# Attention products in float32 instead of high and low parts, two heads side by side in the array

## The chip, the cores and the metric

The kernel runs on one core of one Trainium2 chip. A core has TensorE (matrix products, results in PSUM), VectorE, ScalarE and GpSimd for element-wise work, and SyncE (SP), whose queue issues the DMAs. Time is device microseconds from start to end of one execution. Before the change it is 2203.7 us, the median of three runs (2202.99 to 2203.8).

## The reference

An attention layer with a compressed memory, then a mixture of eight experts and a plain two-layer network. Cut to what matters here:

```python
B, H, S, D = (4, 8, 576, 64)
scores = scale * np.matmul(q, k.transpose(0, 1, 3, 2))
scores = np.where(causal, -1000000000.0, scores)
scores = scores - scores.max(-1, keepdims=True)
a = np.exp(scores)
a /= a.sum(-1, keepdims=True) + 1e-09
local = np.matmul(a, v)
q_p = phi(q)                                  # elu + 1
mem_ret = np.einsum('bhsd,bhde->bhse', q_p, M_prev)
mem_norm = np.einsum('bhsd,bhd->bhs', q_p, z_prev)[..., None] + 1e-06
g = 1.0 / (1.0 + np.exp(-beta))[None, :, None, None]
x = g * (mem_ret / mem_norm) + (1 - g) * local
# then: gate of x with 8 rounds of row and column normalization,
# 8 experts of 512 -> 1024 -> 512 on all 2304 tokens, and 512 -> 2048 -> 512
```

All arrays are float32.

## The kernel before

Heads go in pairs: 4 batches of 4 pairs are 16 pairs, the two heads of a pair on partitions 0 to 63 and 64 to 127. `Attention.run` is a generator that records the work of one pair after the other; `yield` hands back control, so that the caller can put other work in between.

**Precision.** The products are made of operands in float32r, a float32 of fewer bits. Each operand `x` is cut into a high part (`hi`, a copy into a float32r tile, mostly on ScalarE) and a low part (`lo = x - hi`, on GpSimd or VectorE), and a product of two operands is the sum of high by high, high by low and low by high. `split` does it for q and k (lines 131 to 141), `values` for v and the memory matrix (175 to 185), `turned` for the features, `turn` for the probabilities.

**One pair** runs through four stages of query rows: blocks 0 and 1 of 128 rows, block 2, block 3, and the last 64 rows of both heads (`STAGES`). In a stage, `turn` transposes the probabilities of the pair before (TensorE into `atps`), with the high part taken out by ScalarE (`ath`) and the low part by VectorE (`atl`); `scores` makes the products of this pair into `sps`; `softmax` adds the mask and finds the row minimum on VectorE (line 214) and takes exponentials with row sums on ScalarE (line 216). The scores of heads 0 and 1 use 64 rows of the array each:

```python
for i, (x, y) in enumerate(((qh, kh), (qh, kl), (ql, kh))):
    for j in range(2):
        s, o = slice(j * D, (j + 1) * D), 512 * j + 256 * n
```

For the last stage both heads' 64 queries stand as a block-diagonal matrix `bd`, on all 128 rows. After the stages `normalize` divides by the row sums (lines 220 to 227; its first instruction writes `sm`, once a pair). `outputs` multiplies for the pair before, one head at a time: the stationary operand is 128 columns wide, 64 of v's high part and 64 of its low part, so the high parts' sum comes out on one half of the partitions and the low parts' on the other, and `collect` adds the halves into `x` (lines 279 and 285). `turned` transposes the features `nq` into `tps` (line 170).

**What sets the order.** The engines take their instructions in the order of a scheduler that runs over the recorded program. Pairs 0 to 3 run with nothing but the weight conversion of the first expert beside them (`W`, lines 465 and 466). From then on each `yield` of the attention lets `fill` put in up to two units of the first expert's work (`First.run`: `ph`, line 499, and `po`, line 507; four units are a step on 256 tokens), as the table says:

```python
FILL = {1: 1, 2: 2, 4: 2, 5: 2, 7: 2}
```

A pair of heads so takes 16 units, 4 steps. Of First's 72 steps 48 stand beside the attention; the others stand in the gate and the normalization after it. Then come the other experts (`rest`, lines 812 to 881), which take most of the time and are not touched.

Of the kernel before, what the change touches and what calls it, by code (L numbers as in the profile page):

```python
# [60 lines left out]
class Attention:  # L61
# [6 lines left out]
    def __init__(self, tc, ctx, xh, xl, xd, qt, kt, qn, vn, M_prev, z_prev, ident, g_bc, iomg_bc):  # L68
# [25 lines left out]
        self.at = [self.sb.tile([P, 2, self.WIDE], F32R, name=f"at{part}") for part in "hl"]  # L94
        self.qk = {n: [self.sb.tile([P, S], F32R, name=f"{n}{part}") for part in "hl"] for n in "qk"}
        self.bd = [self.sb.tile([P, P], F32R, name=f"bd{part}") for part in "hl"]
        self.ms = [self.sb.tile([P, P], F32R, name=f"ms{j}") for j in range(2)]
        for t in self.bd:
            nc.gpsimd.memset(f32(t), 0.0)
        for j, t in enumerate(self.ms):  # L100
            nc.gpsimd.memset(f32(t[D - j * D:P - j * D]), 0.0)
        for t in self.at:
            nc.vector.memset(f32(t[:, :, 1024:1152]), 0.0)
            nc.vector.memset(f32(t[:, :, 1344:1472]), 0.0)
# [7 lines left out]
    def load_qk(self, r):  # L112
        for nm, src in (("q", self.qt), ("k", self.kt)):
            r["raw" + nm] = self.sbt([P, S], "raw" + nm)
            self.nc.sync.dma_start(out=r["raw" + nm], in_=src[r["b"], r["hp"]])
# [8 lines left out]
    def load_v(self, r):  # L124
        b, hp = r["b"], r["hp"]
        r["v"] = self.sbt([P, 2, 5, D], "nv")
        self.nc.sync.dma_start(out=r["v"], in_=self.vn[b, hp])
        r["m"] = self.sbt([P, D], "nm")
        self.nc.sync.dma_start(out=r["m"], in_=self.M[b, 2 * hp:2 * hp + 2].rearrange("h p d -> (h p) d"))

    def split(self, r):

        nc = self.nc
        for n in "qk":
            (hi, lo), raw = self.qk[n], r["raw" + n]
            nc.scalar.activation(hi, raw, AF.Copy)
            nc.gpsimd.tensor_sub(lo, raw, f32(hi))
        for t, x in zip(self.bd, self.qk["q"]):
            for j in range(2):
                s = slice(j * D, (j + 1) * D)  # L140
                nc.gpsimd.tensor_copy(t[s, s], f32(x[s, 512:]))
# [33 lines left out]
    def values(self, r):  # L175

        nc = self.nc
        vs = r["vs"] = self.sbt([P, 10, P], "vs", F32R)
        v = r["v"].rearrange("p j c d -> p (j c) d")
        nc.vector.tensor_copy(vs[:, :, :D], v)  # L180
        nc.gpsimd.tensor_sub(vs[:, :, D:], v, f32(vs[:, :, :D]))
        for j, ms in enumerate(self.ms):
            s = slice(j * D, (j + 1) * D)
            nc.gpsimd.tensor_copy(ms[s, :D], r["m"][s])
            nc.gpsimd.tensor_sub(ms[s, D:], r["m"][s], f32(ms[s, :D]))

    def scores(self, r, ts):
# [3 lines left out]
        (qh, ql), (kh, kl) = self.qk["q"], self.qk["k"]  # L191
        if ts == (4,):
            qh, ql = self.bd
            for o, k0, kn in ((192, 0, 320), (512, 320, 256)):
                for i, (x, y) in enumerate(((qh, kh), (qh, kl), (ql, kh))):
                    nc.tensor.matmul(ps[:, o:o + kn], x, y[:, k0:k0 + kn], start=(i == 0), stop=(i == 2))
            return
        for n, t in enumerate(ts):
            w = max((t + 1) * P, 256)
            for i, (x, y) in enumerate(((qh, kh), (qh, kl), (ql, kh))):  # L200
                for j in range(2):
                    s, o = slice(j * D, (j + 1) * D), 512 * j + 256 * n
                    nc.tensor.matmul(ps[:, o:o + w], x[s, t * P:(t + 1) * P], y[s, :w], start=(i == 0), stop=(i == 2))
# [29 lines left out]
    def turn(self, r, ts):  # L233
# [26 lines left out]
    def outputs(self, r, j):  # L260
        nc = self.nc
        av = r["av"] = self.big("avps")
        rows = slice(j * D, (j + 1) * D)
        vs, ms, at = r["vs"], self.ms[j], self.at

        def group(o, q0, nq, parts):
            for i, p in enumerate(r["pT"]):
                nc.tensor.matmul(av[:, o:o + nq], ms, p[:, q0:q0 + nq], start=(i == 0), stop=False)
            for i, (c, s0, sn) in enumerate(parts):
                for k, t in enumerate(at):  # L270
                    nc.tensor.matmul(av[:, o + nq - sn:o + nq], vs[:, 5 * j + c, :], t[:, j, s0:s0 + sn], start=False,  # L271
                                     stop=(i == len(parts) - 1 and k == 1))

        group(256, 0, 256, ((0, 1600, 256), (1, 1344, 256)))
# [901 lines left out]
```

## Time and profile before

| | before |
|---|---|
| median of the runs | 2203.7 us |
| the profiled execution | 2206.66 us, span 2204.9 us |
| TensorE busy | 2131.9 us, 97% |
| VectorE busy | 1498.6 us, 68% |
| ScalarE busy | 821.8 us, 37% |
| GpSimd busy | 1183.0 us, 54% |
| mean granted TensorE clock | 0.987 |

PE is TensorE's products, PEld its weight loads, DVE VectorE, ACT ScalarE, POOL GpSimd. A row `avps<-ath,vs` names the tile that is written and those that are read. The shares over the whole span say little on the change, since the attention ends at 387 us; the stretches before that have to be read by themselves. An instruction's busy time holds its latency, and products overlap, so the distance between two starts is what a product costs. A true float32 product stands as two records in the trace.

### The profile page before, as it was taken

To read this page: it belongs to the slowest core of one execution; us is meant where nothing else is said; L and a number is where in the kernel's file an instruction comes from. 1 tells how busy PE (TensorE), PEld (TensorE's weight loads), DVE (VectorE), ACT (ScalarE), POOL (GpSimd) and SP (SyncE) were. 2 spreads that over 40 slices of the span, in tenths; PEclk is the share of its full clock that TensorE was granted. 3 is DMA by queue.
4 is the path that set the end of the run, shared out by engine and by line. 5 is a ranking of instruction groups with operands and counts; after the bars stand their busy time and mean duration, and the time that the engine had idled before them with its cause. 6 is when DMAs were issued, how large, how long until landed. Compare 5 with 4: busy or idle time off the path is not lost.

```text
span 2204.9 us, 35500 instructions
## 1 busy us (share of the span) xinstructions
PE 2131.9 (97%) x13781; PEld 1899.0 (86%) x13781; DVE 1498.6 (68%) x2666; ACT 821.8 (37%) x1645; POOL 1183.0 (54%) x1151
## 2 busy tenths in 40 slices
PE   5799999889999999999999999999999999999999
PEld 4688888789888899899889989889889898888998
DVE  7977776648776777777776898755555553566565
ACT  6777776233332222222222333333322333332421
POOL 7545443356774544444444678855554544564550
PEclk8899999999999999999999999999999999999999
DMA  4333331234532212212225444411111151326111
GB/s 148 99 100 104 106 107 54 82 107 153 154 119 67 67 58 72 88 58 67 68 68 205 159 136 125 131 58 58 39 58 58 39 221 58 114 89 237 57 58 39
DMA packets 161512, 214.17 MB, mean 97 GB/s; under 512 B 11072, under 2 KB 108352, under 8 KB 159808
## 3 DMA queue, kind: packets, MB, share of 16 engines
q1 hardware_dynamic: 161344, 211.90, 30.2%
q8 instruction: 109, 1.79, 0.3%
q14 instruction: 59, 0.48, 0.1%
HBM read 162.55 MB, written 49.28 MB: 96 GB/s over the span
## 4 chain that ended last, share of the span: by engine, by line
PE 74%; DVE 5%; issue 3%; POOL 3%; ACT 1%; DMA 1%; POOLq 0%; DVEq 0%; ACTq 0%
PE po L867 37%; PE pq L824 28%; PE pq L812 4%; PE po L507 1%; PE ph L499 1%; PE avps L271 1%; DVE hl L843 1%; POOL w0l L614 0%; DMA xa<-xd 0%; DVE acc L877 0%; DVE c L845 0%; PE atps L247 0%; DVE c L834 0%; POOL ql L614 0%; PE xt L929 0%
## 5 line engine op out<-in xcount | busy, mean ns | idle before, releaser
L867 PE MATMUL po<-w,hh 128*128 128x512 f32 x2592 | 810.6, 393 | 9.0 <-DVE acc L877 4.1
L867 PEld LDWEIGHTS po<-w,hh 128*128 128x128 f32 x2592 | 473.9, 188 | 107.3 <-DVE acc L877 3.4
L867 PE MATMUL po<-w,hl 128*128 128x512 f32 x1296 | 509.3, 393 | 0.0
L614 POOL TENSOR_TENSOR w0l<-raw,w0h 128x512 fp32r<-128x512 f32 x144 | 191.3, 1349 | 360.2 <-ACT w0h L613 359.7
L842 ACT ACTIVATE hh<-c 128x512 fp32r<-128x512 f32 x224 | 129.2, 624 | 477.5 <-DVE c L837 477.5
L867 PEld LDWEIGHTS po<-w,hl 128*128 128x128 f32 x1296 | 243.5, 188 | 56.1
L824 PE MATMUL pq<-Xh,w0h 128*128 128x256 f32 x960 | 266.2, 277 | 2.2 <-DVE uv L832 1.4
L824 PE MATMUL pq<-Xl,w0h 128*128 128x256 f32 x960 | 265.3, 276 | 0.0
L824 PE MATMUL pq<-Xh,w0l 128*128 128x256 f32 x960 | 265.1, 276 | 0.0
L843 DVE SCALAR_TENSOR_TENSOR hl<-c,hh 128x512 fp32r<-128x512 f32 x224 | 169.6, 798 | 79.2 <-ACT hh L842 79.2
L877 DVE SCALAR_TENSOR_TENSOR acc<-po,Pm,acc 128x512 f32<-128x512 f32 x252 | 178.4, 748 | 48.9 <-PE po L867 47.0
L614 POOL TENSOR_TENSOR w<-raw,w 128x512 fp32r<-128x512 f32 x144 | 199.8, 1405 | 3.3 <-ACT w L613 3.3
L832 DVE TENSOR_TENSOR uv<-pq,s 128x256 f32<-128x256 f32 x144 | 60.4, 420 | 193.8 <-ACT s L831 193.5
L824 PEld LDWEIGHTS pq<-Xh,w0h 128*128 128x128 f32 x960 | 180.1, 188 | 7.3 <-DVE uv L832 1.8
L824 PEld LDWEIGHTS pq<-Xl,w0h 128*128 128x128 f32 x960 | 180.2, 188 | 4.2
L824 PEld LDWEIGHTS pq<-Xh,w0l 128*128 128x128 f32 x960 | 180.2, 188 | 0.0
L831 ACT ACTIVATE s<-pq 128x256 f32<-128x256 f32 x144 | 54.8, 381 | 255.5 <-PE pq L824 255.4
L614 POOL TENSOR_TENSOR ql<-raw,qh 128x512 fp32r<-128x512 f32 x48 | 62.6, 1325 | 131.3 <-ACT qh L613 131.3
L846 ACT ACTIVATE hh<-c 128x512 fp32r<-128x512 f32 x64 | 40.5, 632 | 185.7 <-DVE c L845 185.7
L824 PE MATMUL pq<-Xh,w1h 128*128 128x256 f32 x384 | 106.1, 276 | 1.1 <-ACT xa L942 1.1
L824 PE MATMUL pq<-Xl,w1h 128*128 128x256 f32 x384 | 106.0, 276 | 0.0
L824 PE MATMUL pq<-Xh,w1l 128*128 128x256 f32 x384 | 106.0, 276 | 0.0
(274 smaller groups left out, 5395.8 us busy)
## 6 DMA issues: line engine op xcount, KB each, us to landing
raw<-in_moe_w_dram SPq DMA_DIRECT2D x136, 512.0 KB, 3.6
Xh<-kh SPq DMA_DIRECT2D x6, 1792.0 KB, 7.5
Xl<-kl SPq DMA_DIRECT2D x6, 1792.0 KB, 11.6
f<-in_moe_w_in_dram SPq DMA_DIRECT2D x16, 512.0 KB, 5.0
f<-in_moe_w_out_dram SPq DMA_DIRECT2D x16, 512.0 KB, 4.9
raw<-wide_in SPq DMA_DIRECT2D x16, 512.0 KB, 3.8
raw<-wide_out SPq DMA_DIRECT2D x16, 512.0 KB, 3.8
kh<-sth SPq DMA_DIRECT2D x12, 512.0 KB, 5.1
```

What stands on the lines that cost most here:

```text
L271: nc.tensor.matmul(av[:, o + nq - sn:o + nq], vs[:, 5 * j + c, :], t[:, j, s0:s0 + sn], start=False, stop=(i == len(parts) - 1 and k == 1))
L499: nc.tensor.matmul(ph[:, :T], wp[:, c, f0:f0 + P], x[:, c, t0:t0 + T], start=(n == 0), stop=(n == 11))
L614: self.nc.gpsimd.tensor_sub(lo, src, f32(hi))
L812: nc.tensor.matmul(ph[:, f * SB:(f + 1) * SB], wp(a, c % 2), xp[x][:, c], start=(n == 0), stop=(n == 11))
L824: nc.tensor.matmul(b[-1][:, o:o + SB], wp(a, c), X[s][part][:, x, c], start=(n == 0), stop=(n == 5))
L831: nc.scalar.activation(s1, b[0][:, lo], AF.Copy)
L832: v.tensor_add(uv[:, 0], b[0][:, up], s1)
L842: nc.scalar.activation(hh[:, f], c, AF.Relu)
L843: v.scalar_tensor_tensor(out=hl[:, f], in0=c, scalar=0.0, in1=f32(hh[:, f]), op0=ALU.max, op1=ALU.subtract)
L846: nc.scalar.activation(hh[:, f], c, AF.Copy)
L867: nc.tensor.matmul(po[j], a[:, f, r], w[1, part][:, f], start=(fp == 0 and f == 0 and n == 0), stop=(fp == 1 and f == 1 and n == 2))
L877: nc.vector.scalar_tensor_tensor(out=acc[t], in0=po[j], scalar=Pm[:, t0 + t, e:e + 1], in1=acc[t], op0=ALU.mult, op1=ALU.add)
```

## The change

All attention products are made with float32 operands, in one product where there were two or three. `split`, `values`, `collect` and the low parts are gone. q, k, v and the memory matrix are used as they are loaded, in two buffers each; `bd` is loaded from memory instead of copied. The scores keep the row halves, but with blocks cut to their own width (128 columns where 256 were taken). The outputs of both heads go into one `av` tile, head 0 in columns 0 to 63 of the array and head 1 in columns 64 to 127, each with its own moving operand; one copy by ScalarE takes both heads' `x`. Of the four evacuations of transposed probabilities VectorE makes two, ScalarE two.

```diff
-        self.at = [self.sb.tile([P, 2, self.WIDE], F32R, name=f"at{part}") for part in "hl"]
+        self.at = self.sb.tile([P, 2, self.WIDE], F32, name="at")
+        self.bd = [self.sb.tile([P, P], F32, name=f"bd{i}") for i in range(2)]
+        self.ms = [[self.sb.tile([P, D], F32, name=f"ms{j}{i}") for j in range(2)] for i in range(2)]
...
     def load_qk(self, r):
+            r[nm] = self.sbt([P, S], nm, bufs=2)
+            nc.sync.dma_start(out=r[nm], in_=src[b, hp])
+        r["bd"] = self.bd[hp % 2]
+        for j in range(2):
+            s = slice(j * D, (j + 1) * D)
+            nc.sync.dma_start(out=r["bd"][s, s], in_=self.qt[b, hp, s, 512:])
...
-        hi, lo = r["pT"] = [self.sbt([P, S], "pT" + part, F32R) for part in "hl"]
-        nc.scalar.activation(hi, ps[:, P:P + S], AF.Copy)
-        nc.vector.tensor_sub(lo, ps[:, P:P + S], f32(hi))
+        r["pT"] = self.sbt([P, S], "pT")
+        nc.scalar.activation(r["pT"], ps[:, P:P + S], AF.Copy)
...
     def scores(self, r, ts):
-            w = max((t + 1) * P, 256)
-            for i, (x, y) in enumerate(((qh, kh), (qh, kl), (ql, kh))):
-                for j in range(2):
-                    s, o = slice(j * D, (j + 1) * D), 512 * j + 256 * n
-                    nc.tensor.matmul(ps[:, o:o + w], x[s, t * P:(t + 1) * P], y[s, :w], start=(i == 0), stop=(i == 2))
+            w = (t + 1) * P
+            for j in range(2):
+                s, o = slice(j * D, (j + 1) * D), 512 * j + 256 * n
+                nc.tensor.matmul(ps[:, o:o + w], q[s, t * P:(t + 1) * P], k[s, :w], start=True, stop=True)
...
-        hi, lo = (to(t) for t in self.at)
-        nc.scalar.activation(hi, src, AF.Copy)
-        return lambda: nc.vector.tensor_sub(lo, src, f32(hi))
+        if ts in ((0, 1), (3,)):
+            return lambda: nc.vector.tensor_copy(to(self.at), src)
+        nc.scalar.activation(to(self.at), src, AF.Copy)
...
+    def outputs(self, r):
         def group(o, q0, nq, parts):
-            for i, p in enumerate(r["pT"]):
-                nc.tensor.matmul(av[:, o:o + nq], ms, p[:, q0:q0 + nq], start=(i == 0), stop=False)
+            for j in range(2):
+                nc.tensor.matmul(av[j * D:(j + 1) * D, o:o + nq], r["ms"][j], r["pT"][:, q0:q0 + nq], start=True, stop=False)
             for i, (c, s0, sn) in enumerate(parts):
+                for j in range(2):
+                    nc.tensor.matmul(av[j * D:(j + 1) * D, o + nq - sn:o + nq], r["v"][:, j, c, :], at[:, j, s0:s0 + sn], start=False, stop=i == len(parts) - 1)
-        group(256, 0, 256, ((0, 1600, 256), (1, 1344, 256)))
-        group(512, 256, 320, ((0, 64, 320), (1, 384, 320), (2, 704, 320), (3, 1088, 256), (4, 0, 64)))
+        group(256, 0, 256, ((0, 1600, 256), (1, 1472, 128)))
+        group(512, 256, 320, ((0, 64, 320), (1, 384, 320), (2, 704, 320), (3, 1152, 192), (4, 0, 64)))
+        nc.scalar.activation(x, av[:, 256:256 + S], AF.Copy)
+        nc.vector.tensor_copy(xh, x)
...
     def run(self):
-                self.split(nxt)
...
-                self.collect(prev, 0)
...
-                self.outputs(prev, 1)
-                self.collect(prev, 1)
...
-            self.values(r)
```

How the instructions stand now, at three places (`x2` at a row's end: two such instructions in a row). On TensorE, scores of the fourth pair, blocks 2 and 3, with transposes for the pair before between them; before:

```order
L203 MATMUL sps<-kh,qh 128x384 x2
L203 MATMUL sps<-kl,qh 128x384 x2
L203 MATMUL sps<-kh,ql 128x384 x2
L247 MATMUL atps<-ident,a_835 128x128 x4
L247 MATMUL atps<-ident,a_838 128x128 x4
L203 MATMUL sps<-kh,qh 128x512 x2
L203 MATMUL sps<-kl,qh 128x512 x2
L203 MATMUL sps<-kh,ql 128x512 x2
```

and the same place now, to the end of the pair's scores:

```order
L179 MATMUL sps<-k,q 128x384 x2
L223 MATMUL atps<-ident,a_650 128x128 x4
L223 MATMUL atps<-ident,a_653 128x128 x4
L179 MATMUL sps<-k,q 128x512 x2
L215 MATMUL atps<-ident,a_673 128x128 x5
L173 MATMUL sps<-k,bd_127 128x320
L173 MATMUL sps<-k,bd_127 128x256
```

Three pairs of products have become one pair, head 0 and head 1 in turn; the transposes stand where they stood.

On TensorE, the second group of outputs (320 query columns), with `ms` the memory matrix and `vs` or `nv` the values; before, of one head:

```order
L268 MATMUL avps<-pTh,ms_134 128x320
L268 MATMUL avps<-pTl,ms_134 128x320
L271 MATMUL avps<-ath,vs 128x320
L271 MATMUL avps<-atl,vs 128x320
L271 MATMUL avps<-ath,vs 128x320
L271 MATMUL avps<-atl,vs 128x320
L271 MATMUL avps<-ath,vs 128x320
L271 MATMUL avps<-atl,vs 128x320
L271 MATMUL avps<-ath,vs 128x256
L271 MATMUL avps<-atl,vs 128x256
L271 MATMUL avps<-ath,vs 128x64
L271 MATMUL avps<-atl,vs 128x64
```

and now, of both heads:

```order
L242 MATMUL avps<-pT,ms_131 64x320
L242 MATMUL avps<-pT,ms_132 64x320
L245 MATMUL avps<-at,nv 64x320 x6
L245 MATMUL avps<-at,nv 64x192 x2
L245 MATMUL avps<-at,nv 64x64 x2
```

High and low have become head 0 and head 1, and the second head's run of the same length, which stood behind some fill, is gone.

On VectorE, from the last of `normalize` to the first softmax of the next pair, with fill (`hl`); before:

```order
L225 TENSOR_SCALAR a_1271<-a_1271,sm 128x384
L285 TENSOR_TENSOR x<-avps,x 64x576
L512 SCALAR_TENSOR_TENSOR hl<-ph,hh 128x256
L180 CAST vs<-nv 128x10x64
L285 TENSOR_TENSOR x<-avps,x 64x576
L173 TENSOR_TENSOR pTl<-tps,pTh 128x576
L288 CAST xh<-x 128x576
L258 TENSOR_TENSOR atl<-atps,ath 128x2x384
```

and now:

```order
L201 TENSOR_SCALAR a_984<-a_984,sm 128x384
L201 TENSOR_SCALAR a_987<-a_987,sm 128x384
L253 CAST xh<-x 128x576
L468 SCALAR_TENSOR_TENSOR hl<-ph,hh 128x256
L233 COPY at<-atps 128x2x384
```

The two adds, the cast of v and the low part of the features are gone, and the evacuation of the transposes no longer reads a second tile that ScalarE writes.

## Rows read from the trace of the kernel before

**Rows 1.** The page, busy tenths in 40 slices of 55.1 us each.

```profile
PE   5799999889999999999999999999999999999999
...
DVE  7977776648776777777776898755555553566565
```

**Rows 2.** VectorE in time, first instruction of `normalize`, once a pair (start us, us).

```profile
20.75 0.17 DVE L220 SCALAR_TENSOR_TENSOR sm<-sm,inv 128x9 f32<-128x9 f32 x1 [1.61 <-POOL ms L184]
...
100.35 0.25 DVE L220 SCALAR_TENSOR_TENSOR sm<-sm,inv 128x9 f32<-128x9 f32 x1
...
127.68 0.17 DVE L220 SCALAR_TENSOR_TENSOR sm<-sm,inv 128x9 f32<-128x9 f32 x1 [0.94 <-ACT a L216]
...
365.08 0.17 DVE L220 SCALAR_TENSOR_TENSOR sm<-sm,inv 128x9 f32<-128x9 f32 x1
```

**Rows 3.** Stretches: from:to, us, busy of PE, PEld, DVE, ACT, POOL (instructions), PEclk, DMA, GB/s.

```profile
20.70:100.35 79.65, 59.08 (x366) 48.09 (x367) 75.11 (x158) 62.29 (x136) 48.84 (x65) 0.82 0.40 118
...
127.68:365.08 237.40, 233.76 (x1673) 202.94 (x1673) 186.31 (x460) 172.00 (x378) 113.10 (x144) 1.00 0.34 99
```

**Rows 4.** TensorE in time with fill (start us, us, line, tiles, shape, count).

```profile
214.99 0.50 PE L203 MATMUL sps<-kh,qh 64*128 64x512 f32 x2
215.33 0.40 PE L203 MATMUL sps<-kl,qh 64*128 64x512 f32 x2
215.56 0.39 PE L203 MATMUL sps<-kh,ql 64*128 64x512 f32 x2
215.89 0.73 PE L507 MATMUL po<-w,hh 128*128 128x512 f32 x2
...
217.39 0.71 PE L239 MATMUL atps<-ident,a 128*128 128x128 f32 x5
...
218.75 0.41 PE L196 MATMUL sps<-kh,bdh 128*128 128x320 f32 x1
...
219.65 0.28 PE L499 MATMUL ph<-xh,w0h 128*128 128x256 f32 x1
...
221.06 0.28 PE L268 MATMUL avps<-pTh,ms 128*128 128x256 f32 x1
...
223.32 0.70 PE L507 MATMUL po<-w,hh 128*128 128x512 f32 x2
...
224.80 0.28 PE L268 MATMUL avps<-pTh,ms 128*128 128x256 f32 x1
...
227.05 0.77 PE L170 MATMUL tps<-ident,nq 128*128 128x128 f32 x5
...
229.05 0.82 PE L247 MATMUL atps<-ident,a 128*128 128x128 f32 x6
...
230.72 0.28 PE L203 MATMUL sps<-kl,qh 64*128 64x256 f32 x2
230.84 0.28 PE L203 MATMUL sps<-kh,ql 64*128 64x256 f32 x2
```

**Rows 5.** Line 397, a float32 product (ns min/median/max, first and last start, form).

```profile
L397 PE MATMUL csum<-cs,ones x16: 172/256/383, 414.0 to 462.0; 128*128 128x8 f32 x16
```

**Rows 6.** VectorE's groups, 55 to 385 us (count, busy us, mean ns, idle before).

```profile
L258 DVE TENSOR_TENSOR atl<-atps,ath 128x768 fp32r<-128x768 f32 x28 | 26.7, 954 | 7.9 <-ACT ath L257 7.6
...
L285 DVE TENSOR_TENSOR x<-avps,x 64x576 f32<-64x576 f32 x29 | 21.9, 754 | 11.6 <-ACT x L279 11.5
...
L258 DVE TENSOR_TENSOR atl<-atps,ath 128x640 fp32r<-128x640 f32 x15 | 12.3, 821 | 11.4 <-ACT ath L257 11.4
...
L173 DVE TENSOR_TENSOR pTl<-tps,pTh 128x576 fp32r<-128x576 f32 x14 | 10.6, 758 | 1.4 <-ACT pTh L172 1.0
...
L180 DVE CAST vs<-nv 128x640 fp32r<-128x640 f32 x14 | 7.3, 520 | 10.7 <-PE avps L271 10.7
```

**Rows 7.** TensorE in time, first pair.

```profile
12.54 0.58 PE L203 MATMUL sps<-kl,qh 64*128 64x256 f32 x2 [4.95 <-POOL kl L137]
```

**Rows 8.** Weight loads in time, outputs with fill.

```profile
221.07 0.19 PEld L268 LDWEIGHTS avps<-pTl,ms 128*128 128x128 f32 x1
```

More of the change, by code (lines that the diff above doesn't have):

```diff
@@ L125, in load_v @@
         b, hp = r["b"], r["hp"]
-        r["v"] = self.sbt([P, 2, 5, D], "nv")
+        r["v"] = self.sbt([P, 2, 5, D], "nv", bufs=2)
         self.nc.sync.dma_start(out=r["v"], in_=self.vn[b, hp])
[L128 to L138, printed above, removed]
-            for j in range(2):
-                s = slice(j * D, (j + 1) * D)
-                nc.gpsimd.tensor_copy(t[s, s], f32(x[s, 512:]))
+        r["ms"] = self.ms[hp % 2]
+        for j in range(2):
+            s = slice(j * D, (j + 1) * D)
+            self.nc.sync.dma_start(out=r["ms"][j][s], in_=self.M[b, 2 * hp + j])
     def features(self, r):
@@ L266, in group @@
+        nc.scalar.activation(to(self.at), src, AF.Copy)
+    def outputs(self, r):
+        nc, at = self.nc, self.at
+        av = self.big("avps")
         def group(o, q0, nq, parts):
-            for i, p in enumerate(r["pT"]):
-                nc.tensor.matmul(av[:, o:o + nq], ms, p[:, q0:q0 + nq], start=(i == 0), stop=False)
+            for j in range(2):
+                nc.tensor.matmul(av[j * D:(j + 1) * D, o:o + nq], r["ms"][j], r["pT"][:, q0:q0 + nq], start=True, stop=False)
             for i, (c, s0, sn) in enumerate(parts):
-                for k, t in enumerate(at):
-                    nc.tensor.matmul(av[:, o + nq - sn:o + nq], vs[:, 5 * j + c, :], t[:, j, s0:s0 + sn], start=False,
-                                     stop=(i == len(parts) - 1 and k == 1))
@@ L274, in outputs @@
[L274 to L290 removed]
+                for j in range(2):
+                    nc.tensor.matmul(av[j * D:(j + 1) * D, o + nq - sn:o + nq], r["v"][:, j, c, :], at[:, j, s0:s0 + sn], start=False, stop=i == len(parts) - 1)
@@ L299, in run @@
         self.load_v(pairs[0])
-        self.split(pairs[0])
         self.load_qk(pairs[1])
@@ L316, in run @@
                 yield 2 if k < 3 else 4
-            if nxt is not None:
-                self.split(nxt)
-                if n + 2 < len(pairs):
-                    self.load_qk(pairs[n + 2])
-            if prev is not None:
-                self.outputs(prev, 0)
+            if n + 2 < len(pairs):
+                self.load_qk(pairs[n + 2])
             self.normalize(r)
             if prev is not None:
-                self.collect(prev, 0)
-            yield 5
-            if prev is not None:
-                self.outputs(prev, 1)
-                self.collect(prev, 1)
+                self.outputs(prev)
                 if prev["hp"] == HP - 1:
                     yield ("done", prev["b"])
-            self.values(r)
+            yield 5
             self.turned(r)
@@ L339, in run @@
         for ts in self.STAGES:
-            self.turn(prev, ts)()
+            lo = self.turn(prev, ts)
+            if lo:
+                lo()
             yield 7
-        for j in range(2):
-            self.outputs(prev, j)
-            self.collect(prev, j)
+        self.outputs(prev)
         yield ("done", B - 1)
```

57 lines of the change are left out of this document (12 added, 45 removed).

## The prediction

> **What bounds the kernel now.** I read the busy shares in slices first, then the pair marks on VectorE, then the busy times of the stretches that these marks bound, and last TensorE's own instructions in order of time. The slices [rows 1] show two regimes inside the attention part: in the first two slices of 55 us VectorE is busy 7 and 9 tenths and TensorE 5 and 7; from the third on TensorE stands at 9 and VectorE at 7. The marks are the starts of `sm` (line 220), one for each of the 16 head pairs [rows 2]. From 20.75 to 100.35 us there are four periods of 19.9 us each; from 127.68 to 365.08 us ten periods of 23.74 us. In the first of these stretches [rows 3] VectorE is busy 75.11 of 79.65 us (94%) and TensorE 59.08, at a mean granted clock of 0.82: **VectorE bounds it.** In the second TensorE is busy 233.76 of 237.40 us at clock 1.00 and VectorE 186.31 (78%): **TensorE bounds it**, because the first expert's products are put between the attention's. After 387 us no instruction is changed, and the fill has done the same 48 of 72 steps by then, so what the attention part gains or loses should reach the end whole.
>
> **The prices on TensorE.** A float32r product streams one column in a cycle: a pair of row halves of 512 columns starts 0.23 us after the one before it (215.33 and 215.56), one of 256 columns 0.12 us (230.72 and 230.84) [rows 4]. Each such entry is two matmuls, so the row halves run side by side. A float32 transpose streams slower: six of 128 columns take 0.82 us and five 0.71 (at 229.05 and 217.39), so 0.11 us each, two cycles a column. A true float32 product appears in the trace only at 8 columns: 16 records for the 8 rounds of line 397 [rows 5], so each is two passes. No row shows a long one. The cheapest reading is two passes at one cycle, the dearest two passes at the transposes' two cycles. I take the second, four cycles a column at 2.4 GHz, since the transposes are the only long float32 rows; I keep the first as a rival.
>
> *Scores.* Before, measured from entry to exit: (3,) takes 214.99 to 215.89, 0.90 us; (4,) 218.75 to 219.65, 0.90; (0,1) six pairs of 0.12 and 0.20 of entry and exit (0.90 less three times 0.23), 0.92; (2,) by the same arithmetic 0.72. Sum 3.44 us a pair of heads. After: both heads issue low pass, high pass, in turn. If the array takes instructions in order but lets the two halves overlap, head 1's first pass runs beside head 0's second, and a stage lasts 4N cycles for each block and one pass (2N) more: (0,1) 2048 cycles, (2,) 2304, (3,) 3072, (4,) 2304 with the full array; 9728 cycles or 4.05 us, and 0.7 us of entries. So 4.75, **plus 1.3 us a pair.**
>
> *Outputs.* Before: 221.06 to 223.32 and 224.80 to 227.05, 4.51 us a pair [rows 4]. After: 2176 columns for each head, heads in column halves: 8704 cycles if they overlap and a pass of 512 at the start, 3.84 us, and 0.2 for entry and exit. So 4.04, **minus 0.5 us.** No row of before has a product in column halves; serial heads would take 17408 cycles, 7.25 us. I take the overlap, by the nearest rows, the row halves. Transposes stay, 30 of 0.11 us.
>
> So TensorE pays 0.84 us more for each pair.
>
> **The prices on the others.** VectorE loses for each pair [rows 6] pTl 0.758, the atl of stages (2,) and (4,) 0.954 and 0.821, two adds of x 1.508, the cast of vs 0.520: 4.56 us. The other two subtractions become copies of the same size, priced alike, and wait for one engine fewer. ScalarE loses two copies of q and k, two of the four of the probabilities and one of two x copies; GpSimd loses the subtractions for q, k and v and all small copies. Both have room already. Three more small loads a pair and two fewer waits on GpSimd stand in SP's queue; their data are needed a pair later, and I cost them at nothing. If the cover fails, stage (4,) waits for `bd` some 2 us.
>
> **The sum, against the profiled run's 2206.66 us (span 2204.9).**
>
> *First pair:* TensorE waits 4.95 us for `kl` on GpSimd [rows 7], and that wait goes. VectorE and ScalarE have their features work to do meanwhile; I take minus 4, bounds 0 and minus 7.
>
> *Four periods of VectorE's stretch:* busy 75.11/4 less 4.56 is 14.2 us, and its 1.1 us of idle stays: 15.4. TensorE comes close behind: 4.05, 3.84 and 3.27 us are 11.2, at clock 0.82 13.6, with 0.9 of entries 14.5. Two engines that near each other do not hide each other fully, so I take 15.9: four times minus 4.0, **minus 16.** Bounds: minus 18 (VectorE alone) and minus 8 (a period of 17.9, where they alternate).
>
> *Eleven pairs with fill:* plus 0.84 on TensorE each. Against that stand its waits. The fill of one pair is 4 steps of 12 products at 0.12 and 6 at 0.23, 11.3 us; with 3.44, 4.51 and 3.27 that is 22.5 of 23.74, so 1.2 us a period is waiting. With VectorE at 14 instead of 18.6 us I take 0.84 of it as gone: **0.** Bounds: plus 9 (none goes) and minus 4 (all goes).
>
> The sum is minus 20: 2186.7 for a run like the profiled one. The median of the runs shown is 2203.7, so the forecast is **2184 us**, own range 2175 to 2200.
>
> **A rule against it.** In the trace the weight load of the next product starts with the product before it: the load for `pTl` at 221.07 [rows 8], the `pTh` product at 221.06, on the same rows. A load costs nothing there. The Trainium skill, "TensorE: Matmul & The Clock Gate", Part 3, "What overlaps and what doesn't", says that a weight load overlaps a running matmul only if it goes to other row groups. Column halves share all their rows. By that rule the outputs would show their loads, which is the third rival; by the rows they would not. The trace speaks against the rule for the full array, and is silent on halves.
>
> **The rivals.**
> 1. *Column halves run one after the other.* For it: no row shows them together. Outputs are then 7.45 us, 2.94 over before; with the scores 4.26, less 0.84 of waits, 3.4 a pair, 38 us over eleven. In the first stretch TensorE needs 14.6/0.82 and 0.9, 18.7 us: minus 5. First pair minus 4. Plus 29: **2233 us.** This decides from 1.5 us of outputs beyond before's, where the loss with fill passes the gain ahead of it. If the row halves go serially too, scores cost 1.2 us more: plus 13 and no gain in the first stretch, **2251 us.**
> 2. *TensorE takes VectorE's place.* The clock in the first stretch is a mean of two levels, 1.2 and 2.4 GHz; with longer float32 streams around the same waits it may be lower. At 0.65 the period is 18.1: minus 7, first pair minus 4, plus 9 with fill where the waits stay. **2202 us**, no change. Against it: TensorE would be busier than now, and with fill the clock is 1.00.
> 3. *Each pass shows its weight load.* Entering a half costs 0.11 us (0.34 for the first entry at 214.99 against 0.23). At 36 passes of outputs that is 4.0 us a pair: 44 over eleven pairs, minus 2 and minus 4 before: **2242 us.**
> 4. *A float32 pass is one cycle a column.* Scores and outputs halve, 3.8 us a pair off, which the other engines let through in part: **2150 us.**
>
> **How the numbers follow.** Forecast 0.57; serial columns 0.14, serial rows too 0.05; TensorE in VectorE's place 0.12; loads shown 0.08; one cycle 0.04. The range 2174 to 2238 leaves out the fourth rival, the doubly serial case and half of the third, with the forecast's lower edge some 0.15. About 0.2%, 4.4 us, is what a measurement of this kernel can tell from no change. Faster by more than that: forecast, one cycle and a little of rival 2, 0.62; within it 0.10; slower 0.28.
>
> **What would show it.** Right: the first five marks 16 us apart, VectorE below 15.5 us in each period; a pair of `sps` products of 512 columns ending 1.3 us after its start; the outputs of both heads within 4.1 us between two fill products; the later marks again about 23.7 apart; the first gate product about 20 us earlier than 387. Wrong: outputs over 6 us (columns serial), scores of (3,) at 1.7 (rows serial), a granted clock under 0.7 in the first stretch, or marks with fill over 25 us apart.

## The result, and the profile after

The changed kernel takes 2172.43 us (median of four runs, 2171.12 to 2173.57) against 2203.34 for the kernel before, measured beside it: a ratio of 0.986, 95% interval 0.9843 to 0.9877. The forecast was 2184, with a range of 2174 to 2238; the time lies just below it. The profiled execution took 2173.57 us, its span is 2171.8. The slices of 54.3 us each answer to [rows 1]:

```profile
PE   6999999799999999999999999999999999999999
...
DVE  6756564747777777677776888755555453566565
```

TensorE now stands at 9 from the second slice on but for the eighth, which has 7, and VectorE is nowhere above it. The marks, first instruction of `normalize` on VectorE (start us, us), answer to [rows 2]:

```profile
19.03 0.17 DVE L196 SCALAR_TENSOR_TENSOR sm<-sm,inv 128x9 f32<-128x9 f32 x1 [3.59 <-ACT a L192]
33.15 0.16 DVE L196 SCALAR_TENSOR_TENSOR sm<-sm,inv 128x9 f32<-128x9 f32 x1
50.86 0.16 DVE L196 SCALAR_TENSOR_TENSOR sm<-sm,inv 128x9 f32<-128x9 f32 x1
64.57 0.16 DVE L196 SCALAR_TENSOR_TENSOR sm<-sm,inv 128x9 f32<-128x9 f32 x1
79.23 0.16 DVE L196 SCALAR_TENSOR_TENSOR sm<-sm,inv 128x9 f32<-128x9 f32 x1
...
103.34 0.17 DVE L196 SCALAR_TENSOR_TENSOR sm<-sm,inv 128x9 f32<-128x9 f32 x1 [0.94 <-ACT a L192]
...
335.79 0.17 DVE L196 SCALAR_TENSOR_TENSOR sm<-sm,inv 128x9 f32<-128x9 f32 x1 [0.94 <-ACT a L192]
```

With the first gate product, at 356.01 us instead of 387.01, they give the ledger:

| stretch | before, us | after, us | difference | predicted |
|---|---|---|---|---|
| to the first mark | 20.75 | 19.03 | −1.7 | −4 |
| four periods before the fill | 79.6 | 60.2 | −19.4 | −16 |
| the period in which the fill begins | 27.3 | 24.1 | −3.2 | 0, with the next two |
| ten periods with fill | 237.4 | 232.45 | −5.0 | 0 |
| last mark to the first gate product | 21.9 | 20.2 | −1.7 | 0 |
| the rest | 1817.9 | 1815.8 | −2.1 | 0 |

The rest has no changed instruction; in the experiments below it lay between 1814.1 and 1820.8, so its 2 us are not read as a gain. The attention part gave 31.0 us, of which 9.9 stand where nothing was forecast. The two stretches answer to [rows 3] (busy of PE, PEld, DVE, ACT, POOL, then PEclk):

```profile
19.03:79.23 60.20, 49.35 (x329) 31.17 (x331) 50.66 (x136) 48.25 (x116) 20.85 (x16) 0.90 0.55 160
103.34:335.79 232.45, 228.90 (x1578) 176.35 (x1575) 141.15 (x400) 138.52 (x330) 52.73 (x40) 1.00 0.34 102
```

Before the fill VectorE is busy 84% (before 94) and TensorE 82%: neither bounds alone. With fill TensorE is busy all but 3.55 of 232.45 us, as it was all but 3.64 of 237.40. Its own instructions, with fill, answer to [rows 4]:

```profile
168.13 1.13 PE L179 MATMUL sps<-k,q 64*128 64x512 f32 x4
169.19 0.38 PE L455 MATMUL ph<-xh,w0h 128*128 128x256 f32 x1
...
173.70 0.65 PE L242 MATMUL avps<-pT,ms 128*64 128x256 f32 x4
174.19 0.82 PE L245 MATMUL avps<-at,nv 128*64 128x256 f32 x8
174.84 0.71 PE L242 MATMUL avps<-pT,ms 128*64 128x320 f32 x4
175.37 2.23 PE L245 MATMUL avps<-at,nv 128*64 128x320 f32 x20
177.53 0.39 PE L455 MATMUL ph<-xh,w0h 128*128 128x256 f32 x1
```

Stage (3,), two heads of 512 columns, is four records: two passes for each head. From its start to the next product it lasts 1.06 us (168.13 to 169.19); 0.90 before. Both heads' outputs last 3.83 us (173.70 to 177.53) in place of 4.51. The records of both heads' first passes start at 168.13, those of the second passes at 168.66. So the two heads take their passes beside each other: 512 columns at two cycles and two passes are 0.85 us, plus an entry of about 0.2; the lag of a pass that the prediction took would have made 1.48. The groups for the ten periods with fill say the same. Outputs first, of the kernel before:

```profile
127.68:365.08 237.40, 47.75 (x356) 47.63 (x356) 15.11 (x20) 12.91 (x20) 1.00 0.34 99
```

and after, the stretch restricted to the instructions of `avps`, PE's busy time being the second number:

```profile
103.34:335.79 232.45, 38.97 (x364) 24.28 (x361) 6.51 (x10) 1.00 0.34 102
```

and the same two restricted to `sps`; before, then after:

```profile
127.68:365.08 237.40, 38.14 (x300) 26.24 (x300) 42.50 (x90) 1.00 0.34 99
```

```profile
103.34:335.79 232.45, 41.13 (x200) 18.75 (x200) 42.26 (x90) 1.00 0.34 102
```

Outputs cost TensorE 0.88 us less for each pair, scores 0.30 more: 5.8 us less over ten pairs, where TensorE's whole busy time fell by 4.9 and the stretch by 5.0.

### The profile page after: what moved, and what is told of

Same layout as the page of the kernel before. It is cut to its first block, busy times and chain, and to the rows that moved or that the text cites. A ratio compares the mean times of both kernels' runs of the same rounds, so it can differ in the third digit from the quotient of the medians.

```text
span 2171.8 us, 34844 instructions
## 1 busy us (share of the span) xinstructions
PE 2116.4 (97%) x13621; PEld 1850.0 (85%) x13621; DVE 1412.0 (65%) x2566; ACT 765.4 (35%) x1565; POOL 1076.9 (50%) x977
## 3 DMA queue, kind: packets, MB, share of 16 engines
q1 hardware_dynamic: 164160, 212.43, 30.6%
## 4 chain that ended last, share of the span: by engine, by line
PE 74%; POOL 4%; DVE 4%; issue 3%; DMA 1%; ACT 1%; POOLq 0%; SPq 0%; DVEq 0%; ACTq 0%
PE po L823 37%; PE pq L780 28%; PE pq L768 4%; PE ph L455 2%; PE po L463 2%; DMA xa<-xd 1%; POOL w0l L570 1%; DVE hl L799 1%; POOL stl L628 0%; PE avps L245 0%; PE gps L313 0%; DMA raw<-in_moe_w_dram 0%; PE atps L223 0%; PE sps L179 0%; POOL ql L570 0%
## 5 line engine op out<-in xcount | busy, mean ns | idle before, releaser
L780 PE MATMUL pq<-Xh,sl 128*128 128x256 f32 x384 | 106.1, 276 | 0.0
L780 PE MATMUL pq<-Xh,sh 128*128 128x256 f32 x384 | 106.1, 276 | 0.0
```

What stands on the lines that cost most here:

```text
L780: nc.tensor.matmul(b[-1][:, o:o + SB], wp(a, c), X[s][part][:, x, c], start=(n == 0), stop=(n == 5))
```

## The experiments

The kernel before took 2205.2 to 2206.9 us beside these runs, and the ratios are to it. All start from the changed kernel but the one marked "on before". Costs in the whole time are counted from the changed kernel's 2172.43 us; its second timing, the last row, is 4.0 us higher (the kernel before beside it 3.5 higher), so they can be up to 4 us too large. Stretches as in the ledger, us, from one profiled execution each:

| run | median | ratio, 95% | four early | begin | ten | gate product |
|---|---|---|---|---|---|---|
| heads apart | 2203.01 | 0.9973–0.9992 | 59.0 | 23.5 | 256.5 | 382.2 |
| VectorE's work back | 2187.97 | 0.991–0.9945 | 70.9 | 28.0 | 237.5 | 375.3 |
| the same on scratch | 2199.93 | 0.9963–0.9982 | 72.6 | 26.2 | 238.0 | 378.1 |
| GpSimd's work back | 2188.73 | 0.991–0.9947 | 70.9 | 26.6 | 234.4 | 373.2 |
| both back | 2198.52 | 0.9956–0.9982 | 75.2 | 27.1 | 238.1 | 378.9 |
| GpSimd on scratch | 2241.17 | 1.0141–1.0175 | 123.0 | 23.4 | 232.35 | 422.3 |
| GpSimd tied | 2183.0 | 0.9886–0.9919 | 61.6 | 25.8 | 236.7 | 362.9 |
| features early | 2174.17 | 0.9845–0.9877 | 62.1 | 25.5 | 230.9 | 355.2 |
| scores alone (on before) | 2193.03 | 0.9927–0.996 | 70.3 | 25.8 | 239.5 | 374.5 |
| outputs alone | 2180.66 | 0.9872–0.9902 | 65.8 | 26.0 | 228.7 | 360.7 |
| mixed | 2174.08 | 0.9835–0.9865 | 60.7 | 25.85 | 228.9 | 354.3 |
| changed, again | 2176.41 | 0.9849–0.9882 | 59.1 | 24.8 | 232.4 | 355.5 |

**Heads apart.** Do column halves overlap, or are the outputs short for another reason?

```
             for j in range(2):
                 nc.tensor.matmul(av[j * D:(j + 1) * D, o:o + nq], r["ms"][j], r["pT"][:, q0:q0 + nq], start=True, stop=False)
-            for i, (c, s0, sn) in enumerate(parts):
-                for j in range(2):
+                for i, (c, s0, sn) in enumerate(parts):
```

> The outputs' products of head 0 are all issued before those of head 1 (same products, same column halves, another order). Theory A (TensorE's price counts with fill, and two heads overlap only as neighbours in the queue): the outputs of a pair go from 3.8 to about 7.4 us, eleven pairs with fill pay 3.5 us each and the four early periods 2 us each: about 2172 + 38 + 8 = 2218 us, 2205 to 2228. Theory B (the gain came from relieved waits, TensorE's price hardly counts): within 8 us of 2172. If the array overlaps halves wherever they stand in the queue: outputs stay at 3.8 us and the time at 2172.

Nearly the whole gain goes: 30.6 us over the changed kernel, 26.6 over its second timing. The gate product comes 26.2 us later, all of it from the fill on. The same instructions in another order cost, with `avps` alone, in the ten periods (101.28 to 357.79 us):

```profile
101.28:357.79 256.51, 61.24 (x364) 37.76 (x363) 6.52 (x10) 1.00 0.31 93
```

61.24 us for 38.97: +2.2 a pair, and the period grew by 2.4. Column halves ran side by side only where products of the two heads stood close together in the queue. It is less than two serial heads would cost (7.25 us a pair, by the prediction's cycles; here 6.1), because the seams of the groups still overlap. The first product of head 1, on `pT`, starts beside the last but one of head 0:

```profile
177.55 0.38 PE L244 MATMUL avps<-at,nv 128*64 128x256 f32 x1
177.56 0.43 PE L242 MATMUL avps<-pT,ms 128*64 128x256 f32 x1
```

It does so in the second group too (180.36); the products of head 1 that stand further behind in the queue wait. Before the fill it cost nothing (59.0 for 60.2): there the outputs are not what the others wait for.

**VectorE's work back.** The 4.56 us of VectorE work a pair that the change removed, with results that nothing reads; the first line in stages (2,) and (4,), the third once a head:

```
+        return lambda: nc.vector.tensor_sub(to(self.scr), src, to(self.at))
...
+        nc.vector.tensor_sub(self.sc2[:, :S], ps[:, P:P + S], r["pT"])
...
+            nc.vector.tensor_add(self.sc2[s, :S], av[s, 256:256 + S], x[s])
...
+            nc.vector.tensor_copy(self.sc2, r["v"].rearrange("p j c d -> p (j c d)"))
```

> VectorE's 4.56 us a pair are put back as work whose results nobody reads: the two subtractions from the transposes, the one for pT, the two adds of av and the copy of v. TensorE's products stay. Theory A: the four early periods go back from 15.05 to 18 to 19.5 us, plus 12 to 18, the stretch with fill by 0 to 3: 2184 to 2193 us. Theory B (relief of VectorE is also what the fill stretch gained): plus 5 to 10 more with fill, 2195 to 2203.

It costs 15.5 us in the time. The profiled execution, 2193.41 us, was the slowest of its four, 5.4 over their median; in it the gate product comes 19.3 us later: 10.7 in the four early periods, 3.9 in the next, 5.0 in the ten. So the time is as theory A has it, with less early and more with fill than it said. The early stretch (18.08 to 89.00):

```profile
18.08:89.00 70.92, 53.73 (x333) 35.36 (x335) 64.48 (x160) 49.34 (x117) 21.53 (x17) 0.87 0.47 139
```

VectorE is busy 91% of it again, and a period is 17.7 us. So VectorE's instructions are worth 10.7 of the early gain's 19.4 us. In the ten periods they take back the gain too: TensorE is busy 231.25 us, 2.5 less than before, but idle 6.2 in place of 3.55. So TensorE's shorter work shows there in full only with VectorE relieved.

**The same on scratch.** The same instructions on scratch tiles in SBUF, in place of PSUM, one of them here: is it VectorE's time, or PSUM tiles that are held longer?

```
-        return lambda: nc.vector.tensor_sub(to(self.scr), src, to(self.at))
+        return lambda: nc.vector.tensor_sub(self.scr[:, :n], self.scs[:, :n], self.scs[:, :n])
```

> The same VectorE work as in the run with VectorE's work put back, of the same sizes, but from and to scratch memory: it holds no tile of PSUM and waits for no other engine. Theory V (VectorE's occupied time is what counts): about the same as that run, 2184 to 2190, with plus 7 to 10 in the stretch with fill. Theory H (with two PSUM buffers beside the fill, the later release of the transposes and outputs counts): plus 0 to 3 with fill, plus 8 to 11 early, 2180 to 2184.

It costs no less: 27.5 us in place of 15.5, at the gate product 22.1 in place of 19.3. So the price needs no PSUM to be held. Both theories had less, and the excess is not clean evidence: nothing ties scratch work to its pair, and the order differs. In this run the first of the four early periods alone takes 22.4 us.

**GpSimd's work back.** The subtractions and small copies that GpSimd lost, on q, k, v and M of the same pair, into scratch:

```
+                for m in "qk":
+                    g.tensor_sub(self.scr[:, :S], nxt[m], nxt[m])
+                for j in (0, 1, 0, 1):
+                    s = slice(j * D, (j + 1) * D)
+                    g.tensor_copy(self.scs[s], nxt["q"][s, 512:])
...
+            g.tensor_sub(self.scr, v, v)
```

> GpSimd's removed work is put back (two subtractions of 576 columns, one of 640, eight small ones a pair), results not read. Theory A (VectorE's own work alone made the early gain): within 3 us of 2172. Rival C (part of the early gain, which went beyond the 4.56 us a pair, is VectorE's instructions getting shorter as GpSimd beside them got quieter): VectorE's six scalings go from 2.7 back towards 4 to 5 us, 1.5 to 2 us a period, 2178 to 2182.

It costs 16.3 us, more than either theory had, 10.7 of them early. That looked as if a busy GpSimd were worth as much as VectorE's 4.56 us a pair. But the waits of GpSimd in the early stretch show something that neither kernel has (line, waited for, total us, times, longest):

```profile
POOL scr L288 <- DMA q<-in_qt_dram: 16.3, 4, 6.7
```

The subtraction waits for q of the next pair, 16.3 us in four periods, and the features' scaling by the norm, which TensorE's transposes wait for, is queued behind it. The run had two causes in it, and so has the one with both back.

**Both back.**

> VectorE's and GpSimd's removed work are both put back (results not read), TensorE's float32 products and ScalarE's smaller load stay. If the two engines' relief is the whole gain and adds up: 15.5 and 16.5 us over 2172, 2200 to 2206, as before the change. If both hide in the same gap: 2188 to 2194. What is left to 2206 is TensorE's lower price and ScalarE's.

The edits of the two runs together. The time, 2198.52 us, lies between the two forecasts. Early 75.2 us, 15.0 more than the changed kernel and 4.4 less than before; the two alone would have summed to 81.6, so they overlap. That both delay the same chain of softmax, features and transposes is the likely reason, and is not shown.

**GpSimd on scratch**, to take the wait for q away, and all its other inputs likewise:

```
-                    g.tensor_sub(self.scr[:, :S], nxt[m], nxt[m])
+                    g.tensor_sub(self.scr[:, :S], self.scs[:, :S], self.scs[:, :S])
```

> After, plus the same ten GpSimd instructions a pair as in the run with GpSimd's work put back, at the same places and sizes, but on scratch tiles that wait for no transfer and for no other engine. In that earlier run GpSimd waited 16.3 us of the early stretch for q to be loaded, with the features' scaling queued behind, a wait that neither kernel has. Theory A (a GpSimd that is busy beside VectorE is the price: it lengthens VectorE's scalings and delays the features' scaling behind its own 5 us a period): the four early periods again near 68 us, VectorE's scalings of 384 columns near 1.2 us, the first gate product at 368 or later, the time 2183 to 2189. Rival B (the added wait for q was the price): the scalings may lengthen, but the four periods stay at 60 to 63 us, the gate at 356 to 359, the time at 2172 to 2177.

Slower than before, and no answer to the question. Its GpSimd groups from 17 to 104 us (count, busy us, mean ns):

```profile
L289 POOL TENSOR_TENSOR scr<-scs 128x576 f32<-128x576 f32 x22 | 25.8, 1172 | 1.6
L300 POOL TENSOR_TENSOR scr<-scs 128x640 f32<-128x640 f32 x10 | 12.5, 1252 | 0.8
```

Where 10 and 5 belong stand 22 and 10: with nothing to wait for, the work of later pairs was put ahead of the features' scaling, and TensorE waited for that:

```profile
PE tps L165 <- POOL nq L156: 30.3, 2, 25.4
```

**GpSimd tied.** The same instructions (eleven a pair, where the expectations count ten), reading the last pair's features and outputs, so that they can't move ahead:

```
+                t = r["k"] if prev is None else prev["pT"]
...
+                    g.tensor_sub(self.scr[:, :S], t, t)
...
+                x = prev["x"]
+                g.tensor_sub(self.scr[:, :S], x, x)
```

> The run on scratch tiles didn't answer its question: nothing held its instructions back, and 22 of the large subtractions of 576 columns stood in the first 104 us, where 10 belong. Here the ten GpSimd instructions a pair are tied to the pair by what they read: the four copies and two subtractions that stand for q and k read the last pair's transposed features, those that stand for v and M read the pair's output (576 columns in place of 640), and both are written anew only behind them. They wait for no transfer. Theory A (a GpSimd that is busy beside VectorE is the price): the four early periods at 66 to 72 us, VectorE's scalings longer than in after, the first gate product at 366 or later, the time 2181 to 2190. Rival B (the wait for q, which the first such run added, was the price): the four periods at 60 to 63, the gate at 356 to 360, the time at 2172 to 2178.

It costs 6.6 us against the changed kernel's second timing, 10.6 against the first. The time is theory A's, the gate product in neither range. Early it is the rival's figure, 61.6 us, 1.4 over the changed kernel, so most of the earlier run's 10.7 came with the wait for q. How much of it came through TensorE's clock is not separated: early it was granted 0.79 in that run, 0.94 in this one and 0.90 in the changed kernel. Another 1.7 us stand where the fill begins and 4.3 in the ten periods with fill, which neither theory had placed. In that stretch (106.05 to 342.70):

```profile
106.05:342.70 236.65, 230.96 (x1577) 177.27 (x1574) 144.14 (x400) 138.14 (x330) 113.86 (x144) 0.99 0.33 100
```

TensorE is idle 5.7 us instead of 3.6 and its instructions take 2.1 us more. Of the added idle time, 1.7 us are the fill's wait for the low part of `x`, which GpSimd makes; tied, and in the changed kernel:

```profile
PE ph L471 <- POOL xl L256: 2.8, 2, 1.4
...
PE ph L455 <- POOL xl L255: 1.1, 2, 0.5
```

The longer instructions stand for the most part in one stretch at the lower of TensorE's two clock levels, 1.2 GHz. TensorE had been idle for 1.8 us up to 149.5 and was idle for 0.7 again as the clock fell:

```profile
151.40:154.80 3.40, 3.14 (x9) 2.57 (x10) 1.45 (x7) 1.75 (x6) 1.26 (x1) 0.50 0.61 226
```

At half the clock some 1.7 us are lost. The changed kernel has the same two gaps and keeps its clock. The run with GpSimd's work back and the one with both back have such a stretch too, in the same period. Why the clock falls in these three is open.

VectorE's scaling of the probabilities shows what GpSimd does to it (17 to 104 us, mean ns behind the comma); before:

```profile
L225 DVE TENSOR_SCALAR a<-a,sm 128x384 f32<-128x384 f32 x9 | 11.1, 1263 | 0.0
L225 DVE TENSOR_SCALAR a<-a,sm 128x128 f32<-128x128 f32 x10 | 8.2, 856 | 0.1
...
L225 DVE TENSOR_SCALAR a<-a,sm 128x256 f32<-128x256 f32 x10 | 3.1, 351 | 0.0
```

after:

```profile
L201 DVE TENSOR_SCALAR a<-a,sm 128x256 f32<-128x256 f32 x10 | 6.0, 646 | 0.0
L201 DVE TENSOR_SCALAR a<-a,sm 128x128 f32<-128x128 f32 x11 | 5.0, 461 | 0.0
L201 DVE TENSOR_SCALAR a<-a,sm 128x384 f32<-128x384 f32 x10 | 4.7, 508 | 0.0
```

and with GpSimd's work tied back in:

```profile
L202 DVE TENSOR_SCALAR a<-a,sm 128x256 f32<-128x256 f32 x10 | 7.0, 746 | 0.0
L202 DVE TENSOR_SCALAR a<-a,sm 128x384 f32<-128x384 f32 x10 | 6.5, 694 | 0.0
L202 DVE TENSOR_SCALAR a<-a,sm 128x128 f32<-128x128 f32 x10 | 5.2, 526 | 0.0
```

Two of each a pair: 4.94 us before, 3.23 after, 3.93 tied. The tied instructions lengthen them by 0.7 us a pair, and in the changed kernel VectorE has 2.4 us of idle in a period to take that up.

These means mix two kinds of instruction. In the changed kernel's stretch with fill none is long (ns min/median/max):

```profile
L201 DVE TENSOR_SCALAR a<-a,sm x60: 275/348/417, 104.0 to 314.6; 128x128 f32<-128x128 f32 x20, 128x256 f32<-128x256 f32 x20, 128x384 f32<-128x384 f32 x20
```

From 17 to 104 us 25 of its 31 take 269 to 409 ns, and six 1206 to 1415, whatever their width. Each of the six meets a GpSimd instruction of 1.27 to 1.41 us, and ends 0.08 us (128 columns), 0.15 (256) or 0.22 (384) behind the end of that. One of them:

```profile
33.46 2.50 POOL L422 TENSOR_TENSOR w<-raw,w 128x512 fp32r<-128x512 f32 x2 [7.58 <-ACT w L421]
33.60 1.21 DVE L201 TENSOR_SCALAR a<-a,sm 128x128 f32<-128x128 f32 x1
```

So a scaling that meets a long GpSimd instruction waits until it is over, and what counts is how often they meet: in the same stretch 12 of 29 scalings before, 6 of 31 after, 10 of 30 tied.

**Features early.** TensorE's waits in the early stretch of the changed kernel (line, waited for, total us, times, longest us):

```profile
PE tps L162 <- POOL nq L153: 7.4, 3, 3.2
PE atps L223 <- DVE a L201: 3.9, 1, 3.9
```

The first is for the features' scaling on GpSimd. So second buffers for the features' inputs, loads a pair ahead, and each of their steps a stage earlier:

```
-        r["p"] = self.sbt([P, 5, 2, D], "nq")
+        r["p"] = self.sbt([P, 5, 2, D], "nq", bufs=2)
...
-                if k:
-                    next(f, None)
+                next(f, None)
```

> Not an undoing but a step on: the features' inputs are loaded a pair ahead into two buffers and the features are made a stage earlier, so that the transposes after the outputs no longer wait for GpSimd's scaling (7.4 us in three early pairs). If that wait ends last there: 3 to 7 us less, 2165 to 2169. If VectorE's chain of softmax and scaling ends last anyway: 2172.

No gain: 2174.17 us. The wait went down to 3.7 us, and the other took its place (16.6 to 78.7 us):

```profile
PE atps L223 <- DVE a L201: 5.5, 4, 2.0
PE tps L162 <- POOL nq L153: 3.7, 2, 2.1
```

**Scores alone, outputs alone.** First the kernel before with half the change: `scores`, `load_qk` and no `split` from the changed kernel, outputs as before. Then the changed kernel with the loads, splits and scores of before put back.

> Only the scores are changed to float32 (q, k and bd as loaded), the outputs stay in high and low parts. TensorE pays 0.4 us a pair; ScalarE's two copies and GpSimd's two subtractions and four copies go; VectorE's own work stays. Theory C (quieter GpSimd shortens VectorE's scalings): 5 to 9 us less early, 0 to plus 4 with fill, 2194 to 2202 against 2206 for before on this chip. If VectorE's removed instructions alone count: 2204 to 2210.

> Only the outputs, transposes and values are changed to float32; the scores stay in high and low parts with their split. TensorE gains 0.7 us a pair, VectorE loses its 4.56 us a pair, GpSimd keeps the work for q and k. If the parts add up, the gain is that of the whole change less that of the scores alone: 2176 to 2186. Theory V alone would put all the gain here: 2172 to 2176.

Scores alone save 13 us against before, 1 more than Theory C's range allows; outputs alone 25.5, as forecast. Together that is 38.6, more than the whole change saves: the parts do not add up. Early both help (70.3 and 65.8 for 79.6). The early stretch with the scores alone (17.35 to 87.68):

```profile
17.35:87.68 70.33, 56.72 (x324) 41.40 (x322) 66.41 (x158) 58.18 (x129) 32.56 (x37) 0.88 0.47 138
```

VectorE has the same 158 instructions as before [rows 3], but they keep it busy 66.4 us, not 75.1. That is most of the 9.3 us that this stretch gained. Counted over the four periods, VectorE's instructions take 18.3 us more than the shortest of their form before, 9.4 with the scores alone and 8.0 in the changed kernel. With GpSimd's splits gone, they meet its long instructions less often: 8 of 30 scalings, where 12 of 29 did before. In the ten periods they have opposite signs: scores alone 239.5 for 237.4, outputs alone 228.7. Sum −6.6, together −5.0.

**Mixed.** That points to float32 scores before the fill, and from the sixth pair on the scores of before, with their loads and splits (`scores_hl`):

```
     def scores(self, r, ts):
+        if r["n"] >= 5:
+            return self.scores_hl(r, ts)
```

> After, but only the first five pairs score in float32; from the sixth pair, where the fill begins, scores are again three float32r products of high and low parts, with ScalarE's and GpSimd's splits of q and k (outputs, probabilities and values stay float32 throughout). Theory A (a float32 score costs TensorE 0.39 us a pair more than high and low parts, which counts in full where TensorE bounds, while ahead of the fill GpSimd's relief counts more): the four early periods stay at 60 us as in after, the ten with fill go from 232.5 to 228.7 as with the outputs alone, the first gate product at about 352, and the whole at 2168 to 2170 us, 3 us under after. Rival (the 228.7 with the outputs alone is an order that happened to fit, not the score's price): the ten stay at 231 to 234 and the time at 2171 to 2174. Rival 2 (GpSimd's and ScalarE's splits beside the fill cost what the shorter scores give): the ten at 232, and the rest after the gate longer.

> The changed kernel, word for word, beside the mixed one on the same chip, so that 3 us can be told. Every theory expects 2171 to 2174 us, the four early periods at 60 and the ten with fill at 232 to 233.

The ten periods fall to 228.9 us from 232.4, as theory A expected; its time, 2168 to 2170, does not come. In these periods `sps` takes TensorE 37.00 us, where it takes 41.13 with float32 scores:

```profile
105.14:334.03 228.89, 37.00 (x300) 26.51 (x300) 42.63 (x90) 1.00 0.35 103
```

But the five periods ahead are 2.6 us longer than in the changed kernel beside it, whose own two profiled executions differ by 0.4 there. The gate product comes 1.2 us earlier, and the time, 2174.08 for 2176.41 beside it, is a difference of 0.1% that this measurement does not separate from none.

## Why the prediction was right and wrong

**The bounds** were right. VectorE bounded the early stretch: its work back costs 10.7 us there. TensorE bounded the stretch with fill: where its price changes, the period follows (outputs −0.88 and scores +0.30 a pair gave −0.5; heads apart +2.2 gave +2.4; the scores of before put back, in the mixed run, −0.41 gave −0.35). The gain reached the end whole.

**The step that failed most is the third term, "Eleven pairs with fill: 0".** It measured −9.9 us, where the first term missed by +2.3 and the second by −3.4. Two sizes in it were off, with opposite signs.
- *The price "plus 0.84 on TensorE each".* It measured −0.58 a pair. The scores were put at 4.75 us on the assumption that head 1 lags head 0 by a pass. They do not lag: stage (3,) is 1.06 us from entry to exit where that reading gives 1.48, and the sum of the stages with their busy ends rose by 0.30 instead of 1.3. Outputs fell by 0.88, not 0.5.
- *The relief "1.2 us a period is waiting".* That came from a sum of single prices, 22.5 of 23.74 us. The row on the same stretch [rows 3] already said 3.64 us idle in ten periods, 0.36 each. The missing time lies in the fill: counted from each start to the next, its products take 12.8 us a period, not 11.3, while the transposes take 3.0, not 3.27. Idle stayed at 3.55. Nothing of the 0.84 that was counted on could go.

So TensorE's gain in the ten periods is its shorter work, not fewer waits: busy −4.9, idle −0.1. The period in which the fill begins gave 3.2 us, and it belongs in part to the early stretch: VectorE's work back costs 3.9 there. Two passes at two cycles a column were right: the outputs' 2176 columns make 3.63 us, with 0.2 for entry and exit the 3.83 measured; the lagging pass that the prediction added has no room. At one cycle a column they would take 2.0 us, so the fourth rival fell.

**The second term, four early periods, −16,** measured −19.4, beyond its bound of −18. That bound took VectorE's instructions at their old durations. VectorE's busy time fell from 18.78 to 12.66 us a period, 6.1 and not 4.56; 1.7 of that are the scalings, which met a long GpSimd instruction half as often. The prediction had put GpSimd's relief at nothing ("Both have room already"), and took VectorE's busy time for its own work, though part of it was waiting for GpSimd. Against it, the 1.1 us of idle that was kept became 2.4. VectorE's waits from 19 to 79.2 us:

```profile
DVE a L190 <- PE sps L179: 3.8, 5, 1.5
DVE sm L196 <- ACT a L192: 3.6, 1, 3.6
DVE at L233 <- PE atps L223: 3.5, 4, 1.1
DVE nq L143 <- ACT nq L141: 1.9, 3, 0.8
```

The second lies ahead of the first mark; of the others most are for TensorE, as the "two engines that near each other" of the prediction would have it. The early clock rose from 0.82 to 0.90, so the second rival, a lower clock, fell.

How the early gain splits depends on what else is there. VectorE's removed work costs 10.7 us when it is put back, GpSimd's 1.4 when it is tied to its place and VectorE has room. But the scores alone, which take nothing from VectorE's instructions, gave 9.3 us, since there VectorE bounded and GpSimd's work lengthened its instructions. The share of TensorE, of ScalarE and of the loads no run separates.

**The first term, −4,** measured −1.7, within its bounds of 0 and −7. The 4.95 us wait for `kl` [rows 7] went, and half of it came back in its place: stage (4,) waits for `bd`, as the prediction named for the case that the loads' cover fails.

```profile
13.25 1.28 PE L173 MATMUL sps<-k,bd 128*128 128x320 f32 x4 [2.48 <-DMA bd<-in_qt_dram]
```

**The column halves** overlap, as the prediction took it from the row halves, and the first rival fell. With the heads apart its price appears: had the loop over heads been the outer one, the change would have given 0.2%.

**The weight loads** cost no time that shows: of the outputs' 3.83 us, columns take 3.63, and the third rival's 4.0 us have no room, so it fell. In time, loads of 64 columns with fill:

```profile
173.70 0.20 PEld L242 LDWEIGHTS avps<-pT,ms 128*64 128x64 f32 x4
173.97 0.79 PEld L245 LDWEIGHTS avps<-at,nv 128*64 128x64 f32 x8
```

The second group begins at 173.97, together with the second passes of `pT`; the products that it serves follow at 174.19. The rule of the Trainium skill, "TensorE: Matmul & The Clock Gate", Part 3, "What overlaps and what doesn't", that a load overlaps only other row groups, does not hold for these column halves, which share all rows.

## What to carry to other kernels

Two matmuls in column halves shared the array only where they stood close together in TensorE's queue, so the loop over the halves belongs innermost. Where one engine bounds, read its idle time from the row of the stretch before counting on waits to go; a sum of single prices can leave out as much as the wait it is meant to find. A mean duration can hold waits for another engine: look at the shortest and the longest of the same form too. An experiment that puts work back must read what the old work read and wait for nothing new, and be tied to its place: of three ways to put GpSimd's work back, one added a wait and one let the work run ahead.

## What the runs showed of the hardware that was not expected

- Float32 products of two heads in row halves pay two passes, not three: two heads of 512 columns take 1.06 us, only 0.16 more than the three float32r products of high and low parts (0.90) that they replace.
- VectorE's in-place float32 scaling depends on whether it meets a long GpSimd instruction: 384 columns take 0.41 us when they meet none and 1.42 when they meet one, and 128 columns 0.27 or 1.21 to 1.39 (changed kernel). GpSimd's casts of 64 columns, 0.23 to 0.24 us long, do not lengthen them: beside these, 128 columns take 0.27 to 0.29 and 256 columns 0.34 to 0.35 (kernel before). The Trainium skill, "SBUF — State Buffer", "SBUF: two separate sides", describes a pair of ports that VectorE and GpSimd lock against each other for a whole instruction; the traces agree for GpSimd's long instructions, behind whose end the scaling ends by 0.08 to 0.22 us.
